# Attention, mixture of experts and dense layer in one kernel: early weight fetches, scales a task ahead, and a split on GpSimd

## The chip, the cores and the metric

One core of a Trainium2 chip runs the whole kernel in one launch. The metric is the device time of a run in microseconds (us); the median of the runs counts. A profile is one more execution, recorded instruction by instruction.

## The reference

Three layers follow each other. `a` below is a softmax of `phi` over the sequence.

```python
k_m, v_m = einsum('bhsm,bhsd->bhmd', a, k), einsum('bhsm,bhsd->bhmd', a, v)   # 8 x 8 heads, 576 x 64, 32 slots
x = softmax(q @ k_m.T / 8) @ v_m                    # -> x: 4608 tokens x 512
logits = x @ w_gate                                 # 8 experts, 576 tokens each, greedy by order of logits
out[mask_e] = relu(x[mask_e] @ w1[e]) @ w2[e]       # w1 512 x 1024, w2 1024 x 512, float32
h = out @ w_in;  g = h * clip(h + 3, 0, 6) / 6      # w_in 512 x 2048
y = g @ w_out                                       # w_out 2048 x 512
```

The expert that is filled first is chosen by the data, so its weights can be fetched only once the routing has found its index.

## The kernel before, in words

**Precision.** Matmuls run in float16 with each float32 operand split in a high and a low half (`hi = fp16(s*x)`, `lo = fp16(s*x - hi)`), three products for one. Weights and activations are first multiplied by a power of two found from their squares or their maximum.

**Stages.** The attention runs to about 240 us. Then the experts come in the order in which the routing finds them: `route(k)` is a chain of small steps between DVE and PE that ends in `ei{k}` (row numbers of the expert's weights) and `ix{k}` (its tokens). `gathers()` fetches the tokens' rows of x by five indirect DMAs from GpSimd and transposes them into `xt`. `l1(k)` and `l2(k)` are the expert's layers, 192 matmuls of 288 columns each. The result `y` (two tiles [128, 2, 576]; 512 columns are used here, the other 64 of all eight experts are collected into a ninth group) goes through `ysplit(k)`, and `unit(k)` is the dense layer of that group in eight steps: seven products `pq`/`pr` of six matmuls with 256 columns, then four pieces `acc` of six matmuls with 512 columns. The order is l1(0), l2(0), l1(1), l2(1), units 0 and 1, l1(2), l2(2), l1(3), l2(3), unit 2 and so on to units 6, 7 and 8.

**Weights of the experts.** `weights()` goes through 16 tasks T = 2k + which (which = 0: w1, 1: w2). For each it fetches four tiles `wst0` to `wst3` of [128, 1024] float32 by indirect DMA from GpSimd (`w_issue`), squares them on ACT, finds the scale (`pow2`), waits until the layer of the expert before no longer needs the float16 tiles, and converts eight halves: ACT writes the high half, DVE the low half (of three halves in tasks 1 to 3 GpSimd writes the low one, `PS`). As a tile is converted, `w_later` fetches the next task into it.

**Dense weights.** w_in and w_out arrive as 64-bit numbers. `dense_max()` takes the maximum of the last blocks, `dense()` loads 32 pieces in the order `PO` into buffers `dst` and rebuilds float32 numbers from them: ACT one or two copies, DVE two or three integer steps, paced by `turn()`. Pairs of w_in pieces become one of eight blocks `wid` in DRAM (`wino_weights`: sums on DVE, splits on ACT and GpSimd, two writes `wga`, `wgb`), which `stream()` reads back as `ws` for every step of every unit. w_out pieces become the resident tiles `wo` in slots 16 to 31.

**Order.** The instructions of each engine are put in order by a planner: generators wait for planned times and conditions while PE's work advances the clock `CK.now`; `V_`, `A_` and `G_` stand for DVE, ACT and GpSimd with a planned time `t`; `spawn(task, lim)` lets a task go on when its engine is planned to be free within `lim` us. The planner decides the order alone; on the chip each engine runs its list and waits for data.

**`ysplit(k)`** takes the maximum of y, finds a scale `s`, forms four sums of quarters of y on DVE (unscaled), and of seven operands writes the high half on ACT (`scale=s`) and the low half on DVE (`(src*s) - hi`).

Of the kernel before, what the change touches and what calls it, by code (L numbers as in the profile page):

```python
# [8 lines left out]
F32 = mybir.dt.float32  # L9
# [10 lines left out]
def attn_moe_kernel(ctx: ExitStack, tc: tile.TileContext, q, k, v, phi, w_gate, w1, w2, w_in, w_out, out):  # L20
# [677 lines left out]
    nc.gpsimd.iota(pb, pattern=[[1, 4]], base=512 * E, channel_multiplier=4, allow_small_or_imprecise_dtypes=True)  # L698
    tid = rt.tile([128, NT], I32, name="tid")
# [53 lines left out]
    IDX, EIX, SX = {}, {}, {}  # L753
# [14 lines left out]
    def route(k):  # L768
# [145 lines left out]
        EIX[k] = ei  # L914
        yield V_.t - 0.3
# [106 lines left out]

    def w_later(T, c):
        yield V_.t + HOP, G_
        w_issue(T, c)

    def weights():
        for T in range(2 * E):
            k, which = divmod(T, 2)
            while k not in EIX:  # L1030
                yield CK.now + 0.3
            for c in range(4):
                w_issue(T, c)
                yield CK.now + 0.8, G_
            while not XD[0]:
                yield CK.now + 0.1
            sq = rt.tile([128, 4], F32, name="wsq", bufs=2)
            for c in range(4):
                st, ready = WST[T, c]
                yield ready, A_  # L1040
                scr = wk.tile([128, 1024], BF16, name="wscr")
                A_.activation(scr, st, AF.Square, accum_out=sq[:, c:c + 1])
# [8 lines left out]
            (S1, S2)[which][k] = s  # L1051
            while k and (L1D, L2D)[which].get(k - 1, 0) < (8, 4)[which]:
                yield CK.now + 0.3
            tl, rd = [], []
            for n in range(9):
                if (k > 3 or T == 4) and n:
                    yield CK.now + (3.0 if k > 3 else 1.2), A_
                if n < 8:
# [3 lines left out]
                    cs = slice(i * 512, i * 512 + 512)  # L1062
                    if n in PS.get(T, ()):
                        A_.activation(WST[T, c][0][:, cs], WST[T, c][0][:, cs], AF.Copy, scale=s[:, 0:1])
                        yield A_.t - 0.3
                        A_.activation(tl[c][:, 0, cs], WST[T, c][0][:, cs], AF.Copy)
                    else:
                        A_.activation(tl[c][:, 0, cs], WST[T, c][0][:, cs], AF.Copy, scale=s[:, 0:1])
                    rd.append(A_.t + HOP)
                if n and n - 1 in PS.get(T, ()):  # L1070
                    yield rd[n - 1], G_
                    c, i = divmod(n - 1, 2)
                    cs = slice(i * 512, i * 512 + 512)
                    G_.tensor_tensor(tl[c][:, 1, cs], WST[T, c][0][:, cs], tl[c][:, 0, cs], op=OP.subtract)
                    yield (CK.now + 0.1, A_) if k > 1 else max(CK.now + 0.1, V_.t - 0.5)
                    WC[T] = c + i, tl
                elif n:
                    yield (rd[n - 1], V_) if k > 1 else rd[n - 1]
                    c, i = divmod(n - 1, 2)
                    cs = slice(i * 512, i * 512 + 512)  # L1080
# [720 lines left out]
```

## Time and profile before

| | |
|---|---|
| median of 3 runs | 1469.22 us (1468.58 to 1472.0) |
| profiled execution | 1465.18 us, span 1463.40 us |
| PE busy | 1335.5 us (91%) |
| DVE, ACT, POOL busy | 949.7 (65%), 818.9 (56%), 484.6 us (33%) |
| mean granted TensorE clock | 0.972 of full speed |
| DMA | 206.29 MB, mean 141 GB/s |

PE is TensorE, DVE VectorE, ACT ScalarE, POOL GpSimd, SP SyncE. Line L568 is the wrapper that issues nearly every instruction of DVE, ACT and POOL after the attention, L622 the one for matmuls, so groups are told apart by their tiles: `w<-wst` is a conversion, `wscr<-wst` a square, `p` an expert layer, `pq`, `pr` and `acc` a unit, `h` the activations of a layer or a unit, `cv`, `cva`, `wga`, `wgb`, `wo` the dense weights. In brackets a timeline gives the idle time before an instruction and what ended it.

### The profile page before, as it was taken

The page shows a single profiled execution, that of the slowest core. Times are in us where ns is not written, and L with a number is a line of the kernel's source. Part 1 is how long each engine was busy: PE and PEld are TensorE (multiplying, and loading weights), DVE is VectorE, ACT ScalarE, POOL GpSimd, SP SyncE. Part 2 cuts the span into 40 slices and gives each one's busy share as a digit, 9 for nine tenths or more (in the row PEclk, how much of TensorE's full clock was granted, in tenths as well). Part 3 has the DMA queues.
Part 4 walks back from the last instruction along what each step waited for, and adds up shares of the span by engine and source line. Part 5 has one row for each costly group of instructions (what it writes and reads, how often), then busy time and mean ns, then how long its engine had stood idle before and what let it go on. Part 6 is the DMA issues. An engine that isn't in the chain of part 4 may idle for free.

```text
span 1463.4 us, 27894 instructions
## 1 busy us (share of the span) xinstructions
PE 1335.5 (91%) x11132; PEld 1001.6 (68%) x11132; DVE 949.7 (65%) x2232; ACT 818.9 (56%) x1560; POOL 484.6 (33%) x530
## 2 busy tenths in 40 slices
PE   4778886987999999989899999999999999999998
PEld 3667665866765667877568767876786687666664
DVE  4687975778898888885875687476246424435322
ACT  3667655468687455554654565465437524545543
POOL 5775312145353343302332323323212211232323
PEclk9989997899999999999999999999999999999999
DMA  9984487446773353313332333234223202243321
GB/s 296 309 273 144 158 263 247 145 142 240 248 236 150 109 183 109 104 60 113 109 133 88 119 105 134 91 109 147 81 66 119 101 30 75 81 144 116 107 99 54
DMA packets 83490, 206.29 MB, mean 141 GB/s; under 512 B 11040, under 2 KB 41760, under 8 KB 83360
## 3 DMA queue, kind: packets, MB, share of 16 engines
q1 hardware_dynamic: 68192, 151.55, 30.6%
q0 software_dynamic: 15168, 52.96, 11.1%
q8 instruction: 87, 1.43, 0.4%
q14 instruction: 43, 0.35, 0.1%
HBM read 177.23 MB, written 27.26 MB: 140 GB/s over the span
## 4 chain that ended last, share of the span: by engine, by line
PE 56%; DVE 6%; issue 5%; ACT 2%; DMA 1%; POOL 1%; POOLq 0%; SPq 0%; ACTq 0%
PE acc L622 21%; PE p L622 16%; PE pq L622 10%; PE pr L622 8%; DVE h L568 1%; ACT h L568 1%; DMA wst<-in_moe_w_dram,ei 1%; PE xp L627 1%; DVE w L568 1%; DVE B L568 0%; DVE C L568 0%; PE rtp L838 0%; POOL h L568 0%; DMA ws<-wid 0%; POOL out_dram L568 0%
## 5 line engine op out<-in xcount | busy, mean ns | idle before, releaser
L622 PE MATMUL acc<-wo,h 128*128 128x512 f16 x1728 | 425.0, 380 | 0.3 <-DVE wo L568 0.2
L622 PEld LDWEIGHTS <-w 128*128 128x128 f16 x3072 | 338.2, 122 | 70.8 <-DVE w L568 8.1
L622 PEld LDWEIGHTS <-ws 128*128 128x128 f16 x3024 | 292.2, 98 | 109.8 <-issue 24.4
L568 POOL TENSOR_TENSOR h<-h,h 128x512 f16<-128x512 f32 x144 | 176.6, 1232 | 425.1 <-ACT h L568 300.5
L622 PEld LDWEIGHTS <-h 128*128 128x128 f16 x1728 | 166.3, 98 | 138.7 <-issue 2.3
L622 PE MATMUL p<-h,w 128*128 128x288 f16 x1536 | 206.2, 290 | 10.9 <-DVE w L568 3.9
L622 PE MATMUL p<-xt,w 128*128 128x288 f16 x1536 | 209.3, 291 | 7.3 <-POOL w L568 2.2
L568 ACT ACTIVATE h<-h,half_c,inv 128x512 f32<-128x512 f32 x144 | 116.5, 811 | 175.4 <-DVE h L568 147.3
L568 DVE SCALAR_TENSOR_TENSOR h<-h,h 128x512 f32<-128x512 f32 x144 | 102.4, 713 | 69.8 <-ACT h L568 69.5
L568 ACT ACTIVATE h<-pq,swv 128x256 f32<-128x256 f32 x216 | 101.4, 470 | 63.7 <-PE pq L622 60.4
L568 POOL DMA_INDIRECT wst<-in_moe_w_dram,ei x64 | 65.2, 1018 | 190.7 <-ACT y L568 50.5
L568 ACT ACTIVATE h<-p 128x288 f16<-128x288 f32 x128 | 52.3, 409 | 127.5 <-PE p L622 126.0
L568 DVE SCALAR_TENSOR_TENSOR h<-pr,swv,h 128x256 f32<-128x256 f32 x144 | 69.1, 480 | 84.1 <-PE pr L622 78.1
L568 DVE SCALAR_TENSOR_TENSOR h<-p,h 128x288 f16<-128x288 f32 x128 | 57.5, 453 | 67.9 <-ACT h L568 64.6
L568 DVE SCALAR_TENSOR_TENSOR w<-wst,s,w 128x512 f16<-128x512 f32 x119 | 97.3, 825 | 1.1 <-ACT w L568 1.1
L568 ACT ACTIVATE h<-h 128x512 f16<-128x512 f32 x144 | 89.4, 621 | 8.3 <-DVE h L568 8.2
L568 ACT ACTIVATE w<-wst,s 128x512 f16<-128x512 f32 x119 | 82.7, 712 | 5.7 <-DVE s L568 5.7
L568 ACT ACTIVATE wscr<-wst 128x1024 bf16<-128x1024 f32 x64 | 67.4, 1053 | 15.3 <-DMA wst<-in_moe_w_dram,ei 14.9
L568 ACT ACTIVATE y<-p 128x288 f32<-128x288 f32 x64 | 25.5, 409 | 87.5 <-PE p L622 79.9
L568 DVE TENSOR_REDUCE ym<-y 128x1 f32<-128x288 f32 (+1 forms) x66 | 30.7, 472 | 62.0 <-ACT y L568 61.7
L568 POOL DMA_INDIRECT xg<-xd,ix x35 | 35.9, 1027 | 102.2 <-DVE ix L568 44.5
L568 POOL DMA_INDIRECT out_dram<-y,ix x36 | 36.7, 1019 | 83.1 <-ACT y L568 79.3
(550 smaller groups left out, 2194.3 us busy)
## 6 DMA issues: line engine op xcount, KB each, us to landing
ws<-wid SPq DMA_DIRECT2D x72, 896.0 KB, 4.6
dst<-in_moe_w_out_dram SPq DMA_DIRECT2D x28, 512.0 KB, 5.3
qt<-in_q_dram SPq DMA_DIRECT2D x8, 1024.0 KB, 13.2
dq<-in_moe_w_in_dram SPq DMA_DIRECT2D x16, 512.0 KB, 4.8
xd<-xs SPq DMA_DIRECT2D x32, 256.0 KB, 5.5
dst<-in_moe_w_in_dram SPq DMA_DIRECT2D x16, 512.0 KB, 4.3
kvt<-in_k_dram SPq DMA_DIRECT2D x7, 1152.0 KB, 11.3
kvt<-in_v_dram SPq DMA_DIRECT2D x7, 1152.0 KB, 12.4
```

What stands on the lines that cost most here:

```text
L568: r = f(*a, **kw)
L622: nc.tensor.matmul(o, l, r, start=start, stop=stop, skip_group_check=more)
L627: nc.tensor.transpose(o, i, idn)
```

## The change

Tasks 1, 2 and 3 are fetched by a task of their own, `w_first`. Tasks 1 and 3 (w2 of experts 0 and 1) go as eight half tiles [128, 512] into slots 24 to 31, the room of w_out's last eight tiles; a new index tile `e8` addresses half rows. Task 2 (w1 of expert 1) uses the four `wst` tiles. The squares and scales of all tasks become a task `scales()`, and `weights()` only converts. In `ysplit` y is multiplied by `s` in place on DVE (two instructions); the high halves are plain copies, and for all groups but the first the sums and low halves go to GpSimd. Three loads of dense blocks are issued by GpSimd instead of SyncE; `dense_max` and `dense` start when the gathers of expert 0 are issued, not at the first eviction of xt; pieces of w_out from the ninth on wait until w2 of expert 1 is converted; and some planned times change.

```diff
+            e8 = rt.tile([128, 8], I32, name="e8", bufs=2)
+            V_.scalar_tensor_tensor(e8, cm.to_broadcast([128, 8]), -1024.0, pb8, op0=OP.mult, op1=OP.add)
...
     def w_issue(T, c):
-        if k not in EIX or (T, c) in WST:
+        if k not in EIX or (T, c) in WST or T in (1, 2, 3):
             return
...
+    def w_first():
+        for T in (1, 2, 3):
+            while not (XR if T == 1 else W1 if T == 2 else W2):
+                yield CK.now + 0.1
+            while not (0 in XI if T == 1 else 1 in EIX if T == 2 else 1 in XI):
+                yield CK.now + 0.1
+            for n in range(4 if T == 2 else 8):
+                yield CK.now, G_
+                c, i = divmod(n, 2)
+                if T == 2:
+                    st = wk.tile([128, 1024], F32, name=f"wst{n}")
+                    G_.indirect_dma_start(out=st, out_offset=None, in_=wv[0], in_offset=U(ap=EIX[1][:, n:n + 1], axis=0))
+                    WST[T, n] = st, dma(1.5, G_.t)
+                else:
+                    st = slot(24 + n, [128, 512], F32, f"wsh{n}_")
+                    G_.indirect_dma_start(out=st, out_offset=None, in_=w28,
+                                          in_offset=U(ap=EI8[T // 2][:, n:n + 1], axis=0))
...
-    def weights():
+    def scales():
         for T in range(2 * E):
...
+            before = T - 1 if T > 4 else T - 2
+            def free(c):
+                return T < 4 or WC.get(before, (0,))[0] > c
...
+            hf = 2 if T in (1, 3) else 1
...
-                yield ready, A_
+                yield ready + (2.5 if 0 < T < 4 else 0.0), A_
...
+                        A_.activation(scr[:, i * 512:i * 512 + 512], w_src(T, 2 * c + i), AF.Square,
+                                      accum_out=sq[:, 2 * c + i:2 * c + i + 1])
...
+    def weights():
+        for T in range(2 * E):
+            k, which = divmod(T, 2)
+            while k not in (S1, S2)[which]:
+                yield CK.now + 0.1
...
-        dense_fetch(st, 16 * which + j)
+        dense_fetch(st, 16 * which + j, nc.gpsimd if NEM < DN[0] < NEM + 4 else nc.sync)
...
     def dense_max():                                   # and in dense()
-        while not GI[0]:
+        while 0 not in XI:
...
-            while not (SDR[which] and spare(1)):
+            while not (SDR[which] and spare(1)) or which and j > 7 and 1 not in W2:
                 yield CK.now + 0.2
-            spawn(dense_piece(which, j, *dload(which, j)), 0.1)
+            spawn(dense_piece(which, j, *dload(which, j)), 0.5 if NB[0] == 4 else 0.1)
...
     def turn():
-        while CK.now < TURN[0] or V_.t > CK.now + 0.05:
+        while CK.now < TURN[0] or V_.t > CK.now + (0.5 if NB[0] == 4 else 0.05):
             yield max(TURN[0], CK.now + 0.05)
-        TURN[0] = CK.now + (1.15 if NB[0] == 4 else 0.85)
+        TURN[0] = CK.now + 0.85
...
-                XDT[0] = dma(0.73, A_.t)
+                XDT[0] = dma(0.73, A_.t) + 1.5
...
-        spawn(ysplit(k), 0.8)
+        spawn(ysplit(k), 0.8 if k else 2.0, k == 0)
...
+        for y in (ya, yb):
+            V_.tensor_scalar(y[:, :, 0:512], y[:, :, 0:512], s, None, op0=OP.mult)
...
-        V_.tensor_tensor(x1, t2, u2, op=OP.add)
-        V_.tensor_tensor(x2, x1, t1, op=OP.subtract)
-        V_.tensor_tensor(t2, t1, t2, op=OP.subtract)
-            A_.activation(ST[k][i][:, 0], src, AF.Copy, scale=s)
-                V_.scalar_tensor_tensor(t[:, 1], src, s, t[:, 0], op0=OP.mult, op1=OP.subtract)
+        Q_ = G_ if k else V_
+        def half(i, src, r):
+            yield r, A_
+            A_.activation(ST[k][i][:, 0], src, AF.Copy)
+            yield A_.t + HOP, Q_
+            Q_.tensor_tensor(ST[k][i][:, 1], src, ST[k][i][:, 0], op=OP.subtract)
+            nl.add(i)
...
+            Q_.tensor_tensor(o, p, q, op=op)
+            spawn(half(i, o, Q_.t + HOP), 0.8 if k else 2.0, k == 0)
...
     spawn(gathers())
+    spawn(scales(), 0.6)
     spawn(weights(), 0.6)
+    spawn(w_first(), 0.6)
```

## Rows read from the trace of the kernel before

**Rows 1.** The page's 40 slices of the span, TensorE, busy tenths
```profile
PE   4778886987999999989899999999999999999998
```

**Rows 2.** Windows: busy us (and count) of each engine per stretch, clock, DMA
```profile
core 0: us, PE busy (x) PEld busy (x) DVE busy (x) ACT busy (x) POOL busy (x), PEclk, DMA share, GB/s
...
260.00:280.00 20.00, 19.79 (x249) 16.90 (x250) 13.87 (x44) 7.23 (x16) 2.22 (x2) 0.87 0.50 164
...
320.00:340.00 20.00, 14.87 (x104) 11.24 (x105) 18.64 (x34) 15.52 (x29) 12.22 (x11) 0.92 0.71 246
...
400.00:420.00 20.00, 19.41 (x134) 13.12 (x134) 19.76 (x37) 18.49 (x37) 12.79 (x10) 1.00 0.85 278
...
420.00:440.00 20.00, 18.94 (x129) 12.52 (x128) 19.55 (x32) 17.52 (x33) 9.49 (x9) 1.00 0.66 218
...
sum 190.00, PE 171.22 PEld 134.26 DVE 164.00 ACT 135.79 POOL 77.18; mean PE 17.12 PEld 13.43 DVE 16.40 ACT 13.58 POOL 7.72
```

**Rows 3.** Timeline of PE, 290 to 390 us: start, us, what, [idle before, releaser]
```profile
298.54 4.77 PE L622 MATMUL p<-h,w 128*128 128x288 f16 x24 [2.36 <-DVE h L568]
...
330.49 0.99 PE L622 MATMUL p<-xt,w 128*128 128x288 f16 x6
...
337.51 3.75 PE L622 MATMUL p<-xt,w 128*128 128x288 f16 x18 [2.21 <-POOL w L568]
...
341.32 20.13 PE L622 MATMUL p<-xt,w 128*128 128x288 f16 x163
...
364.90 0.66 PE L622 MATMUL p<-h,w 128*128 128x288 f16 x2 [3.24 <-ACT w L568]
...
386.54 0.82 PE L622 MATMUL pq<-st__4930,ws 128*128 128x256 f16 x6
```

**Rows 4.** Timeline of POOL (GpSimd): fetches of weights and rows, 290 to 345 us
```profile
297.64 0.96 POOL L568 DMA_INDIRECT wst<-in_moe_w_dram,ei  x1 [1.39 <-DVE sl L568]
...
304.53 0.94 POOL L568 DMA_INDIRECT wst<-in_moe_w_dram,ei  x1 [0.30 <-issue]
...
311.44 1.09 POOL L568 DMA_INDIRECT xg<-xd,ix  x1 [4.78 <-DVE ix L568]
...
332.25 0.97 POOL L568 DMA_INDIRECT wst<-in_moe_w_dram,ei  x1
```

**Rows 5.** Timeline of ACT: first dense piece, first square, conversions of expert 1
```profile
278.98 0.79 ACT L568 ACTIVATE sgn<-dst 128x512 f16<-128x512 f32 x1
...
308.43 1.06 ACT L568 ACTIVATE wscr<-wst 128x1024 bf16<-128x1024 f32 x1 [7.89 <-DMA wst<-in_moe_w_dram,ei]
...
325.12 0.71 ACT L568 ACTIVATE w<-wst,s 128x512 f16<-128x512 f32 x1
...
364.14 0.71 ACT L568 ACTIVATE w<-wst,s 128x512 f16<-128x512 f32 x1
```

**Rows 6.** Chain that ended last, 440 to 470 us: start, us, what
```profile
451.95 2.30 DMA wid<-wgb
454.39 4.37 DMA ws<-wid
458.81 0.83 PE pq L622 x6
```

**Rows 7.** Timeline of SP (SyncE): last writes of x, then dense loads
```profile
236.41 2.51 SPq L429 DMA_DIRECT2D xd<-xs  x3
239.02 2.46 SPq L76 DMA_DIRECT2D dst<-in_moe_w_out_dram  x2
242.45 0.38 SPq L74 DMA_DIRECT2D dst<-in_moe_w_in_dram  x1
```

**Rows 8.** Groups of DVE instructions, 400 to 450 us: busy us, mean ns
```profile
L568 DVE TENSOR_TENSOR sx__5747<-y,sx__5748 128x512 f32<-128x512 f32 x1 | 1.6, 1647 | 0.0
...
L568 DVE SCALAR_TENSOR_TENSOR st__5741<-y,sy,st__5741 128x512 f16<-128x512 f32 x1 | 0.7, 735 | 0.0
...
L568 DVE TENSOR_TENSOR sx__5747<-y,y 128x512 f32<-128x512 f32 x1 | 0.7, 684 | 0.0
```

**Rows 9.** Timeline of POOL, 416 us: the low half of h
```profile
416.10 1.16 POOL L568 TENSOR_TENSOR h<-h,h 128x512 f16<-128x512 f32 x1 [1.81 <-ACT h L568]
```

**Rows 10.** Timeline of PE, 423 us: matmuls that use that h
```profile
423.44 1.46 PE L622 MATMUL acc<-wo,h 128*128 128x512 f16 x6
```

**Rows 11.** Waits of PE over the span: us, times, longest
```profile
PE pr L622 <- DVE h L568: 10.9, 8, 2.6
```

More of the change, by code (lines that the diff above doesn't have):

```diff
@@ L751, in absmax @@
         return m
-    IDX, EIX, SX = {}, {}, {}
+    IDX, EIX, EI8, SX = {}, {}, {}, {}
     SR = [False]
@@ L1031, in weights @@
                 yield CK.now + 0.3
+            before = T - 1 if T > 4 else T - 2
+            def free(c):
+                return T < 4 or WC.get(before, (0,))[0] > c
             for c in range(4):
[L1033 to L1037, printed above, removed]
+                if c == 2:
+                    while not XD[0]:
+                        yield CK.now + 0.1
+                if free(c):
+                    w_issue(T, c)
+                    yield CK.now + 0.8, G_
+            hf = 2 if T in (1, 3) else 1
+            sq = rt.tile([128, 8], F32, name="wsq", bufs=2)[:, 0:4 * hf]
             for c in range(4):
+                while (T, c) not in WST:
+                    if free(c):
+                        w_issue(T, c)
+                    yield CK.now + 0.1
                 st, ready = WST[T, c]
-                yield ready, A_
+                yield ready + (2.5 if 0 < T < 4 else 0.0), A_
                 scr = wk.tile([128, 1024], BF16, name="wscr")
-                A_.activation(scr, st, AF.Square, accum_out=sq[:, c:c + 1])
+                for i in range(hf):
+                    if hf == 2:
+                        A_.activation(scr[:, i * 512:i * 512 + 512], w_src(T, 2 * c + i), AF.Square,
+                                      accum_out=sq[:, 2 * c + i:2 * c + i + 1])
+                        A_.t += 0.15
+                    else:
+                        A_.activation(scr, st, AF.Square, accum_out=sq[:, c:c + 1])
                 yield (CK.now + 3.0, A_) if k > 3 else A_.t + (0.3 if T else -0.1)
@@ L1051, in weights @@
             (S1, S2)[which][k] = s
+    def weights():
+        for T in range(2 * E):
+            k, which = divmod(T, 2)
+            while k not in (S1, S2)[which]:
+                yield CK.now + 0.1
+            s = (S1, S2)[which][k]
             while k and (L1D, L2D)[which].get(k - 1, 0) < (8, 4)[which]:
@@ L1540, in ysplit @@
         ST[k] = [slot(7 * (k % 2) + i, [128, 2, 2, 256], F16, f"st{i}_") for i in range(7)]
-        nl = [0]
+        nl = set()
         x1, x2 = (slot(14 + i, [128, 2, 256], F32, f"sx{i}_") for i in range(2))
-        V_.tensor_tensor(x1, t2, u2, op=OP.add)
-        r1 = V_.t + HOP
-        yield V_.t + 0.5, V_
-        V_.tensor_tensor(x2, x1, t1, op=OP.subtract)
-        r2 = V_.t + HOP
-        yield V_.t + 0.5, V_
-        V_.tensor_tensor(t2, t1, t2, op=OP.subtract)
-        r3 = V_.t + HOP
-        for i, src, r in ((A11, t1, 0.0), (A12, u1, 0.0), (A22, u2, 0.0), (S1Y, x1, r1), (S2Y, x2, r2), (S3Y, t2, r3),
-                          (S4Y, x1, 0.0)):
-            if i == S4Y:
-                V_.tensor_tensor(x1, u1, x2, op=OP.subtract)
-                r = V_.t + HOP
-            yield (max(r, CK.now + (0.9 if k == 2 else 2.0)), A_) if k > 1 else (max(r, CK.now + 2.0 * k), A_)
-            A_.activation(ST[k][i][:, 0], src, AF.Copy, scale=s)
-            def low(t=ST[k][i], src=src):
-                yield (A_.t + HOP, V_) if k > 1 else A_.t + HOP
-                V_.scalar_tensor_tensor(t[:, 1], src, s, t[:, 0], op0=OP.mult, op1=OP.subtract)
-                nl[0] += 1
-            spawn(low(), 0.8)
-            while i in (S1Y, S4Y) and nl[0] < (4, 7)[i == S4Y]:
-                yield CK.now + 0.1
+        Q_ = G_ if k else V_
[5 more added lines that the diff above has]
+            nl.add(i)
+        r = V_.t + HOP
+        for i, src in ((A11, t1), (A12, u1), (A22, u2)):
+            spawn(half(i, src, r), 0.8 if k else 2.0, k == 0)
+            yield CK.now + 0.7, Q_
+        for i, o, p, q, op in ((S1Y, x1, t2, u2, OP.add), (S2Y, x2, x1, t1, OP.subtract), (S3Y, t2, t1, t2, OP.subtract),
+                               (S4Y, x1, u1, x2, OP.subtract)):
+            while i == S4Y and S1Y not in nl:
+                yield CK.now + 0.1
+            yield CK.now, Q_
+            Q_.tensor_tensor(o, p, q, op=op)
+            spawn(half(i, o, Q_.t + HOP), 0.8 if k else 2.0, k == 0)
+            yield Q_.t, Q_
+        while len(nl) < 7:
+            yield CK.now + 0.1
         YR[k] = True
```

28 lines of the change are left out of this document (22 added, 6 removed).

## The prediction

> **What bounds the kernel now.** I read the page's slices first [rows 1]. TensorE (PE) stands at nine tenths or more in every slice of the last third, so nothing there can give much time back; the sixes, sevens and eights lie, but for two, in the first ten slices of 36.6 us, and the attention, which the change leaves alone, takes seven of these. Then I read the stretch behind it window by window [rows 2]: from 320 us on VectorE (DVE) is as full as PE, 19.76 and 19.55 of 20 us at 400 to 440, while between 260 and 280 us it is busy for only 13.87. Over 260 to 450 us it is busy for 164.0 of 190 us, so 26.0 us are free, nearly all before 400.
>
> PE's timeline says what each stage loses [rows 3]. The undisturbed pace is 163 matmuls in 20.13 us, 0.1235 us each. The second layer of expert 0 waits 2.36 us for an eviction on DVE, and its next 24 matmuls take 4.77 us where the pace gives 2.96. The first layer of expert 1 runs from 330.49 to 361.45 us, 30.96 us for 192 matmuls that need 23.7: 7.2 us too long, with a wait on a weight half that GpSimd writes. The second layer of expert 1 then waits 3.24 us for its first converted weights; its 144 matmuls ahead of the dense part need 17.8 us, and the dense part starts at 386.54, 25.1 us after the first layer ended: 7.3 too long.
>
> The weight rows show why [rows 4, 5]. All weights go through one set of four staging tiles, so expert 1's w1 is fetched at 297.64 to 305.5 us, ScalarE (ACT) stands 7.89 us waiting for its landing, and conversion starts at 325.12; w2 of expert 1 is fetched only after that, 332.25 to 341.9, and converted from 364.14.
>
> Last the chain around 450 us [rows 6]: the eighth block of dense-layer weights is written at 451.95, read back at 454.39, and PE gets it at 458.81. So PE runs unit 0 into the end of a second pipeline, the rebuilding of w_in on DVE. Whatever PE gains before 386 us counts only if this pipeline ends earlier too.
>
> **The change part by part.**
>
> *Fetches of tasks 1, 2, 3.* w2 of experts 0 and 1 go into eight half tiles in w_out's slots, w1 of expert 1 into the four staging tiles, free since expert 0's w1 was converted. Task 2's four issues, spread over 7.8 us by waits for these tiles, would take 4 x 1.26 = 5.0 (0.96 busy, 0.30 to the next [rows 4]), and the first no longer stands behind task 1's conversion: I take its landing 6 us earlier (3 to 10). Task 3 no longer waits for task 2's conversion: it follows expert 1's five gathers, which start at 311.44, so it leaves at about 311.44 + 5 x 1.26 = 317.7 instead of 332.25. The price is eight half fetches for four, twice: 8 x 1.26 = 10.1 us of GpSimd time, in a stretch where it is mostly idle (2.22 of 20 us busy at 260 to 280) [rows 2]. What queues behind them on GpSimd are the low halves of w1's conversion, and these have until 330.
>
> *Scales a task ahead.* Squares and power-of-two scale of the next task no longer wait for the conversion of the one before. Eight half squares replace four, twice: each costs between half of a square's 1.06 us and all of it [rows 5], so a task's take 4.2 to 8.5 us instead of 4.2; I take a conversion's 0.71 of the same width, 5.7, 1.5 more, hidden in the time in which ACT waits there now.
>
> *What PE gets back.* Second layer of expert 0: 2.36 + 1.81 = 4.2, I take 4. First layer of expert 1: 7.2, I take 6, since its rows, gathered from 311.44 on, must still land and be copied twice, and are next late. Second layer of expert 1: 7.3, I take 5.5; task 3 issued from 317.7, with task 2's own 10.8 us from first issue to first square and 16.7 from there to conversion [rows 4, 5], converts from about 345, or 350 with the doubled fetches, and the first layer would end at 361.45 - 4 - 6 = 351. Sum 15.5 us at the start of unit 0 (bounds 5 and 19).
>
> *Dense pieces.* Pieces start once the gathers are issued, look 0.5 us ahead instead of 0.05, and follow each other after 0.85 instead of 1.15 us while only four banks serve the expert layers. Their first ACT step is now at 278.98 [rows 5]. Which part of DVE's 26.0 idle us this fills cannot be read off: none at worst, since many gaps are answers awaited from PE; all of it at best. I take a third, 8.7, because the gaps before 320 us are the large ones but belong partly to the routing of expert 1.
>
> *Three loads moved from SyncE to GpSimd.* They leave at 239.02 to 242.8 today, among the last writes of x [rows 7], and the gather of x waits for those writes. On GpSimd they come after the gathers. I take 1 us for the earlier gather (0 to 3). Their issue on GpSimd is not shown: between SyncE's 0.38 and an indirect issue's 1.26 us, at most 3.8 us on an idle engine.
>
> *y scaled in place and split on GpSimd.* For expert 1, in the full stretch 400 to 432, DVE loses four sums and seven low halves: 4 x 0.68 + 7 x 0.74 = 7.9 us [rows 8]. It gains two in-place scalings of 128x1024, not shown before: between 0.68 (a 512-wide row) and twice that, I take 1.0 each. Expert 0 keeps its sums on DVE and pays 2 x 1.0 less 7 x 0.06 = 1.6 us more. The eleven moved instructions cost about 1.16 us each on GpSimd, the length of the h split there [rows 9]: 12.8 us per expert, off the path: unit 1 needs them after the eight blocks of unit 0, whose last starts 72 us after the first [rows 3, 6]. What queues behind them on GpSimd is the low half of h: it ended at 417.26 and the matmuls that use it come some 7 us later, after four of the six matmuls starting at 423.44 [rows 9, 10], so a delay of one or two instructions stays covered.
>
> One thing speaks against this part. On DVE the sum of two SBUF tensors takes 0.684 us in one place and 1.647 in another of the same shape [rows 8], and the long ones lie beside GpSimd instructions. The Trainium skill (SBUF — State Buffer, "Who interferes with whom") says that a DVE instruction with two SBUF inputs and a GpSimd instruction that reads SBUF exclude each other for the whole instruction; by it, eleven more GpSimd instructions could take back up to 12.8 us of DVE time per expert, more than the 7.9 moved. The trace agrees with the lengthening. I count 1.5 us for expert 1 (0 to 11 x 0.96 = 10.6), since only some DVE instructions there have two SBUF inputs. Relief: 7.9 - 2.0 - 1.5 = 4.4 us.
>
> *The sum.* PE's side is 15.5 us earlier at unit 0. The dense side is 8.7 + 4.4 - 1.6 = 11.5 us earlier at the eighth block, and that is the smaller, so it decides; with the gather 12.5. After 470 us, DVE's relief for the later experts touches the 10.9 us in which PE waits for h on DVE [rows 11]: I take 1.5, less 0.5 for collisions. Together 13.5 us. The profiled execution took 1465.18 us (span 1463.40): it becomes 1451.7. The median of the runs is 4.0 us above it, so I forecast 1456 us.
>
> **The rivals.**
>
> *A, the dense pipeline does not move.* DVE's idle time is latency, the relief is eaten by collisions, and PE comes 15 us early to wait at the eighth block. For it: DVE at 99% in [rows 2] and the chain in [rows 6]. Against: the first piece at 278.98 has 40 us of half-empty DVE around it. Only the late 1.5 and the gather stay: 1467 us.
>
> *B, slower: GpSimd locks DVE in the units.* Eight splits (experts 1 to 7 and the leftover one) put 88 instructions beside DVE's joins and products, from 402 us to the end. If one in three holds a DVE instruction for the 0.96 us seen and PE waits for it, 88 x 0.3 x 0.96 = 25 us come back: 1481 us. From 14 such cases on, the whole gain is gone. For it: the lengthened rows in [rows 8], PE's waits on h in [rows 11]. Against: the 7 us of cover in [rows 9, 10], and that the same splits sit on DVE itself today. The exclusion that the Trainium skill states (SBUF — State Buffer, "Who interferes with whom") would be its cause.
>
> *C, more: both pipelines come forward fully.* The stages lose no wait and the dense pieces fill more than half of the idle 26 us: PE's 19 and 5 more from DVE's relief later on, 1445 us or a little below.
>
> **How the numbers follow.** Forecast 0.53, A 0.15, B 0.17, C 0.15. About 0.3%, 4.4 us, is what a measurement of this kernel can tell from no change: faster means below 1464.8, slower above 1473.6. The forecast's own range is 1448 to 1464, nearly all of it faster (0.51, 0.02 the same). A is mostly the same (0.09), in part faster (0.05); 0.01 of it slower. B is slower with 0.15, the same with 0.02. C is all faster. Faster 0.71, same 0.13, slower 0.16. The range reaches from below C to just short of B: 1441 to 1477, with about 0.2 outside.
>
> **What would show it.** Right: no ACT wait of several us for expert 1's w1; its conversion starting near 315 and that of w2 near 350; unit 0 starting near 371 instead of 386.54; the last of the eight dense blocks written near 440 instead of 451.95; DVE fuller before 320 us and below 19 of 20 us at 400 to 440. Wrong: unit 0 early but its eighth step still at 455 or later (A); DVE products of two SBUF tensors over 1 us on average, and PE waits on DVE h above 11 us (B); conversions of expert 1 that start no earlier, because the routing of expert 1 slid behind the early dense pieces, would take the PE side of the sum away.

## The result, and the profile after

The changed kernel took 1486.9 us in the median of four runs (1479.6 to 1487.6), against 1468.9 us for the kernel before beside it (1468.3 to 1472.0): a ratio of 1.0107, 95% interval 1.0072 to 1.0142. It is slower; I had forecast 1456 us, and the time lies above the range. The profiled execution took 1486.16 us with a span of 1484.3, 20.9 more than before.

The slices of the page, TensorE, answer to [rows 1]. The twelfth and thirteenth slice, 408 to 482 us (37.1 us each), read 7 and 8 where [rows 1] has nines; behind them only the 24th and 27th read 8 for 9, and the last 7 for 8.
```profile
PE   4778886978978999989899989989999999999997
```
The windows of after, columns as in [rows 2], whose last three stretches they answer. GpSimd (POOL), the last column before the clock, goes from 9.49 to 20.00 of 20 us at 420 to 440, and PE loses 3 us there, while DVE is hardly relieved (19.55 to 18.77). At 320 to 340 all engines but GpSimd do less than before.
```profile
320.00:340.00 20.00, 12.90 (x76) 9.34 (x75) 10.84 (x21) 12.41 (x22) 15.73 (x15) 0.83 0.72 244
...
400.00:420.00 20.00, 17.34 (x118) 11.38 (x117) 19.34 (x34) 15.44 (x31) 13.20 (x12) 1.00 0.83 252
420.00:440.00 20.00, 15.99 (x108) 10.38 (x107) 18.77 (x23) 16.59 (x30) 20.00 (x16) 0.99 0.53 202
```
PE's timeline of after answers to [rows 3]: unit 0 starts at 386.71, as before (386.54). Expert 1's first layer starts 5.0 us later (335.53 for 330.49), behind a new wait of 4.17 us for gathered rows, and its two layers together win back 4.9. Inside unit 0 PE then waits 5.54 us for a block of w_out, which no row of before showed.
```profile
327.73 1.09 PE L627 MATMUL xp<-ident,xg 128*128 128x128 f32 x4 [4.17 <-DMA xg<-xd,ix]
...
335.53 1.32 PE L622 MATMUL p<-xt,w 128*128 128x288 f16 x8
...
364.28 0.53 PE L622 MATMUL p<-h,w 128*128 128x288 f16 x3
...
386.71 0.82 PE L622 MATMUL pq<-st__5034,ws 128*128 128x256 f16 x6
...
441.53 1.86 PE L622 MATMUL acc<-wo,h 128*128 128x512 f16 x4 [5.54 <-DVE wo L568]
```
The gather, and ACT's first dense piece and conversions, answer to [rows 4, 5]. The first piece is 19 us earlier, but the conversions of expert 1 only 5.4 and 6.1 us, and its gather is 7.6 us later (318.99 for 311.44).
```profile
318.99 0.97 POOL L568 DMA_INDIRECT xg<-xd,ix  x1 [7.29 <-DVE ix L568]
```
```profile
259.70 0.79 ACT L568 ACTIVATE sgn<-dst 128x512 f16<-128x512 f32 x1 [1.59 <-DMA dst<-in_moe_w_in_dram]
...
319.70 0.71 ACT L568 ACTIVATE w<-wst,s 128x512 f16<-128x512 f32 x1
...
358.06 0.74 ACT L568 ACTIVATE w<-wsh__4750,s 128x512 f16<-128x512 f32 x1
```
GpSimd's timeline of after, where [rows 9] had one h split with 1.81 us of idle time before it: sums (sx) and low halves (st) of expert 1 stand between h and the dense blocks (wga), back to back for 25 us. The splits took 1.16 to 1.72 us each.
```profile
419.79 1.34 POOL L568 TENSOR_TENSOR h<-h,h 128x512 f16<-128x512 f32 x1
421.09 1.72 POOL L568 TENSOR_TENSOR sx__5810<-sx__5809,y 128x512 f32<-128x512 f32 x1
422.78 1.15 POOL L568 TENSOR_TENSOR wga<-cva,wga 128x512 f16<-128x512 f32 x1
...
438.67 1.60 POOL L568 TENSOR_TENSOR st__5807<-y,st__5807 128x512 f16<-128x512 f32 x1
440.23 1.60 POOL L568 TENSOR_TENSOR st__5808<-sx__5809,st__5808 128x512 f16<-128x512 f32 x1
441.79 1.15 POOL L568 TENSOR_TENSOR wga<-cva,wga 128x512 f16<-128x512 f32 x1
```
DVE's timeline beside it, against the short and long forms of one shape in [rows 8]: h products at 1.64 and two in 3.20, where one at 415.60 took 0.67.
```profile
415.60 0.67 DVE L568 SCALAR_TENSOR_TENSOR h<-h,h 128x512 f32<-128x512 f32 x1
...
417.33 2.78 DVE L568 TENSOR_TENSOR cva<-cva 128x256 f32<-128x256 f32 x2 [0.46 <-POOL wga L568]
420.04 1.64 DVE L568 SCALAR_TENSOR_TENSOR h<-h,h 128x512 f32<-128x512 f32 x1
...
437.61 3.20 DVE L568 SCALAR_TENSOR_TENSOR h<-h,h 128x512 f32<-128x512 f32 x2
```
The chain that ended last, around the eighth block (start us, us, what), answers to [rows 6]: the read of this block starts at 465.41 instead of 454.39.
```profile
437.69 3.12 DVE h L568 x2
440.81 0.67 DVE wo L568
441.53 1.86 PE acc L622 x4
...
465.41 4.42 DMA ws<-wid
```
PE's waits over the span [rows 11]: the one on h is about as long as before (10.6 for 10.9 us), though DVE was to be relieved; the one on w_out is new.
```profile
PE pr L622 <- DVE h L568: 10.6, 8, 3.1
...
PE acc L622 <- DVE wo L568: 6.4, 3, 5.5
```

### The profile page after: what moved, and what is told of

The parts are those of the page before. It is cut to its first block, busy times and chain, and to the rows that moved or that the text cites. A ratio compares the mean times of both kernels' runs of the same rounds, so it can differ in the third digit from the quotient of the medians.

```text
span 1484.3 us, 27922 instructions
## 1 busy us (share of the span) xinstructions
PE 1345.8 (91%) x11132; PEld 1006.1 (68%) x11132; DVE 949.0 (64%) x2167; ACT 814.2 (55%) x1573; POOL 605.3 (41%) x631
## 4 chain that ended last, share of the span: by engine, by line
PE 62%; DVE 18%; ACT 5%; DMA 5%; issue 4%; POOL 3%; SPq 1%; another core or an unknown queue 0%; POOLq 0%; DVEq 0%; ACTq 0%
PE p L622 19%; PE acc L622 19%; PE pq L622 9%; PE pr L622 7%; DVE h L568 2%; DMA wst<-in_moe_w_dram,ei 2%; PE xa L419 2%; ACT h L568 2%; DVE w L568 2%; PE kvp L190 1%; DVE ql L329 1%; DMA kvt<-in_v_dram 1%; DMA xg<-xd,ix 1%; PE xp L627 1%; DVE C L568 1%
## 5 line engine op out<-in xcount | busy, mean ns | idle before, releaser
L568 POOL TENSOR_TENSOR h<-h,h 128x512 f16<-128x512 f32 x144 | 172.9, 1206 | 331.3 <-ACT h L568 217.6
L568 ACT ACTIVATE h<-h,half_c,inv 128x512 f32<-128x512 f32 x144 | 116.5, 811 | 163.6 <-DVE h L568 141.2
L568 DVE SCALAR_TENSOR_TENSOR h<-h,h 128x512 f32<-128x512 f32 x144 | 114.7, 800 | 69.3 <-ACT h L568 68.8
L568 ACT ACTIVATE h<-pq,swv 128x256 f32<-128x256 f32 x216 | 101.2, 469 | 76.1 <-PE pq L622 73.0
L568 DVE SCALAR_TENSOR_TENSOR h<-pr,swv,h 128x256 f32<-128x256 f32 x144 | 69.2, 481 | 93.1 <-PE pr L622 80.9
L568 ACT ACTIVATE h<-p 128x288 f16<-128x288 f32 x128 | 51.9, 408 | 123.6 <-PE p L622 121.1
L568 POOL DMA_INDIRECT wst<-in_moe_w_dram,ei x56 | 54.4, 972 | 152.5 <-DVE ei L568 70.8
L568 DVE SCALAR_TENSOR_TENSOR h<-p,h 128x288 f16<-128x288 f32 x128 | 57.8, 453 | 66.6 <-ACT h L568 63.3
L568 DVE SCALAR_TENSOR_TENSOR w<-wst,s,w 128x512 f16<-128x512 f32 x109 | 96.2, 888 | 3.3 <-ACT w L568 3.2
L568 ACT ACTIVATE h<-h 128x512 f16<-128x512 f32 x144 | 89.3, 620 | 10.1 <-DVE h L568 9.9
L568 ACT ACTIVATE w<-wst,s 128x512 f16<-128x512 f32 x109 | 76.1, 712 | 7.8 <-DVE s L568 7.8
L568 POOL DMA_INDIRECT xg<-xd,ix x35 | 35.9, 1025 | 101.3 <-DVE ix L568 57.3
L568 ACT ACTIVATE wscr<-wst 128x1024 bf16<-128x1024 f32 x56 | 59.0, 1054 | 31.1 <-DMA wst<-in_moe_w_dram,ei 30.8
L568 POOL DMA_INDIRECT out_dram<-y,ix x36 | 36.4, 1011 | 84.3 <-ACT y L568 73.0
L568 ACT ACTIVATE y<-p 128x288 f32<-128x288 f32 x64 | 25.4, 407 | 81.4 <-PE p L622 63.9
L568 DVE TENSOR_REDUCE ym<-y 128x1 f32<-128x288 f32 (+1 forms) x66 | 30.7, 472 | 56.6 <-ACT y L568 56.3
```

The lines of the kernel that those rows point to most:

```text
L568: r = f(*a, **kw)
```

## The experiments

The ratios are to the kernel before, run beside each on the same chip (medians of before there: 1467.0 to 1469.9 us). "Unit 0" is the time from its first product to that of unit 1, "units 1 to 4" from there to the first product of unit 5, both of the profiled execution. That of the kernel before took 1465.18 us, 2 to 5 us less than its medians here. In every run but e1, e2 and e5 the planner also orders the rest of the kernel anew.

| kernel | median us | ratio, 95% | unit 0 starts | unit 0 | units 1 to 4 |
|---|---|---|---|---|---|
| before | 1468.9 | | 386.5 | 83.7 | 617.1 |
| after | 1486.9 | 1.0107 (1.0072–1.0142) | 386.7 | 92.9 | 627.6 |
| e1 after, no split on GpSimd | 1461.5 | 0.9957 (0.9939–0.9976) | 382.1 | 89.9 | 607.5 |
| e2 after, low halves twice | 1518.4 | 1.0339 (1.0306–1.0372) | 381.9 | 100.7 | 646.3 |
| e3 after, split on DVE | 1489.7 | 1.0146 (1.0120–1.0172) | 385.7 | 99.6 | 618.6 |
| e4 after, y part undone | 1468.6 | 1.0003 (0.9985–1.0021) | 384.7 | 84.5 | 617.3 |
| e5 after, memsets for splits | 1463.7 | 0.9967 (0.9949–0.9985) | 378.5 | 91.8 | 612.9 |
| e6 before + fetches | 1474.0 | 1.0030 (1.0016–1.0044) | 381.9 | 101.8 | 612.6 |
| e7 before + dense pieces | 1450.8 | 0.9874 (0.9847–0.9901) | 386.6 | 78.9 | 609.7 |
| e8 after, no priority | 1480.0 | 1.0080 (1.0050–1.0109) | 386.9 | 81.7 | 630.8 |
| e9 before + y part | 1480.5 | 1.0084 (1.0060–1.0107) | 385.7 | 90.8 | 629.1 |
| e10 before + fetches + dense | 1482.5 | 1.0100 (1.0075–1.0125) | 407.0 | 82.0 | 615.6 |
| e11 before + dense + loads | 1460.7 | 0.9953 (0.9934–0.9972) | 393.4 | 78.8 | 610.0 |
| e12 before + early gate | 1468.4 | 1.0002 (0.9990–1.0015) | 387.5 | 83.8 | 620.7 |
| e13 e7 + fetch of task 3 | 1458.9 | 0.9930 (0.9907–0.9952) | 392.5 | 82.1 | 606.7 |
| e14 before + pace | 1453.1 | 0.9895 (0.9863–0.9927) | 388.3 | 78.9 | 606.6 |
| e15 e7, faster pace | 1473.2 | 1.0030 (1.0012–1.0048) | 397.7 | 83.0 | 612.4 |

### The y part: e1, e2, e5, e3, e4, e8, e9

The y part is what the change does to `ysplit`: scaling in place, plain copies, the split on GpSimd, and expert 0's split ahead of the dense pieces. In e1, e2 and e5 PE, DVE, ACT and SP issue what they issue in the kernel after, in its order (the planner is charged the same cost); only GpSimd's list differs. e1 and e5 leave out the sums and low halves, so they do not compute the layer, and some of their copies and products read another tile.

*e1:*
```
-            Q_.tensor_tensor(ST[k][i][:, 1], src, ST[k][i][:, 0], op=OP.subtract)
+            G_.cost([128, 512])      # k > 0; likewise for the sums
...
-                    mm(banks[b][0], wt[:, blk, wi, c], ST[k][x][:, xi, c], ...
+                    mm(banks[b][0], wt[:, blk, wi, c], ST[k][x][:, 0 if k else xi, c], ...
```


> The kernel after, every instruction of the other engines in the same order, without GpSimd's 88 split instructions (11 for each of experts 1 to 7 and the leftover one): ScalarE still writes the high halves, the products read the high half in place of the low one, the sums are left out. Theory G (GpSimd's new work holds up DVE and GpSimd's own low halves of h and of w_in): most of the loss comes back, 1470 to 1476 us; GpSimd is busy for about 10 of 20 us at 420 to 440 us instead of 20.0; the pairs of w_in's last step take 0.9 us instead of 2.8; the last products of unit 0 start near 460 instead of 469.87; mean of DVE's products of two SBUF tensors back from 800 to about 710 ns. Rival O (the order of the dense pieces and of expert 1's routing is worse, whoever does the splits): 1483 to 1488 us, unit 0 still ends near 479.

*e2:*
```
             Q_.tensor_tensor(ST[k][i][:, 1], src, ST[k][i][:, 0], op=OP.subtract)
+            if k:
+                nc.gpsimd.tensor_tensor(ST[k][i][:, 1], src, ST[k][i][:, 0], op=OP.subtract)
```


> The kernel after with each of the seven low halves of a split issued twice on GpSimd (56 instructions of about 1.16 us more), nothing else changed in any engine's order. Theory G: GpSimd is already full at 420 to 440 us, so unit 0 loses some 8 us more and the later units 1 to 2 us each: 1496 to 1508 us. Rival O: the work is off the path, 1485 to 1490 us.

*e5:*
```
-            Q_.tensor_tensor(ST[k][i][:, 1], src, ST[k][i][:, 0], op=OP.subtract)
+            for n in (256, 256, 128):      # k > 0; likewise for the sums
+                nc.gpsimd.memset(ST[k][i][:, 1, :, 0:n], 0.0)
```


> The kernel after, all orders kept, with each of the 88 split instructions on GpSimd replaced by three memsets (640 values a partition wide each time, no input): the low halves are zero and the sums are left out. GpSimd is about as busy with the splits as in the kernel after (88 x some 1.3 us), but these instructions read nothing. If the loss is the lock (GpSimd's reading instructions and DVE's two-SBUF ones exclude each other): near e1_nosplit, 1461 to 1468 us, mean of DVE's products h<-h,h near 715 ns. If it is GpSimd's queue (low halves of h and of w_in late behind the split): near the kernel after, 1480 to 1490 us, with the means of DVE back but the same waits of PE for GpSimd's halves.

The same group of DVE (L575 is L568 moved by added lines), its 144 products of two SBUF tensors, in e1, e5, after and e2 (busy us, mean ns, then idle time before them):
```profile
L575 DVE SCALAR_TENSOR_TENSOR h<-h,h 128x512 f32<-128x512 f32 x144 | 103.1, 718 | 77.1 <-ACT h L575 76.8
```
```profile
L575 DVE SCALAR_TENSOR_TENSOR h<-h,h 128x512 f32<-128x512 f32 x144 | 103.6, 721 | 79.7 <-ACT h L575 79.1
```
```profile
L568 DVE SCALAR_TENSOR_TENSOR h<-h,h 128x512 f32<-128x512 f32 x144 | 114.7, 800 | 69.3 <-ACT h L568 68.8
L568 DVE SCALAR_TENSOR_TENSOR h<-pr,swv,h 128x256 f32<-128x256 f32 x144 | 69.2, 481 | 93.1 <-PE pr L622 80.9
```
```profile
L568 DVE SCALAR_TENSOR_TENSOR h<-h,h 128x512 f32<-128x512 f32 x144 | 125.1, 873 | 89.6 <-ACT h L568 89.3
```
And the busy line of the page of e1, e5 and after:
```profile
PE 1332.2 (91%) x11132; PEld 1001.4 (69%) x11132; DVE 895.4 (61%) x2167; ACT 814.6 (56%) x1573; POOL 487.8 (33%) x543
```
```profile
PE 1338.6 (92%) x11132; PEld 1003.8 (69%) x11132; DVE 902.4 (62%) x2167; ACT 813.6 (56%) x1573; POOL 605.7 (41%) x807
```
```profile
PE 1345.8 (91%) x11132; PEld 1006.1 (68%) x11132; DVE 949.0 (64%) x2167; ACT 814.2 (55%) x1573; POOL 605.3 (41%) x631
```
With the same 2167 DVE instructions, DVE is busy for 895.4 us without splits, 902.4 beside memsets that keep GpSimd as busy as in after, and 949.0 beside splits that read SBUF. So GpSimd's reading lengthens DVE's work by 46.6 us, and being busy, without reading, by 7.0. DVE's form with one operand in PSUM (pr) stays at 480 ns in all. In time e1 gave back more than expected, e2 cost more, and e5 came out as expected for the lock: within 2.2 us of e1 and 23 us below after. Some of these 23 us are not the splits': up to expert 1's split at 417 us the streams are the same, and yet unit 0 starts 4.6 to 8.2 us earlier in e1, e2 and e5 than in this one execution of after. In it PE stood at the lower of its two granted clocks (0.50 of full speed) from 327.0 to 333.8 us, behind the wait of 4.17 us, and DVE stood for 6.15 us until 265.68, as in e1 and e2 (6.5 and 6.2 us) but not in e5 (2.5 us at most).

From the start of unit 0 to that of unit 5, the reading costs 1.1 + 14.7 = 16 us against e5, and 23 against e1; a second copy of the low halves costs 26 more (e2). So the loss against e5 lies behind unit 0. There PE is idle for 33.0 of 627.4 us in after and for 21.8 of 612.7 in e5, and the wait on h has little part in it. PE's waits in this stretch, first of after, then of e5, are spread over many places; waits on a step of the routing (C) and on converted weights (w) are among those that grew:
```profile
PE pr L622 <- DVE h L568: 8.4, 7, 3.1
...
PE rtp L840 <- DVE C L568: 3.0, 4, 1.4
PE p L622 <- DVE w L568: 2.5, 1, 2.5
```
```profile
PE pr L629 <- DVE h L575: 7.7, 6, 2.4
...
PE rtp L847 <- DVE C L575: 1.4, 1, 1.4
```
e5's memsets need not wait for ACT's high halves, so they may also sit better in GpSimd's queue; its split into reading and waiting is not finer than that. That the added work only costs GpSimd's queue is refuted by e5, and that this order is bad without the splits' work by e1.

*e3:* `Q_ = V_` for all experts.

> The kernel after with the sums and low halves of all experts on DVE, as they were, the in-place scaling kept. Theory G: the lock is gone but DVE gets 11 x 0.7 us per expert back; unit 0's loss mostly comes back, 1470 to 1478 us. Rival O: 1483 to 1490 us, since the dense pipeline and the routing stay as they are.

Theory G missed: no better than after, and inside the range of rival O, which e1 refutes in its turn. Units 1 to 4 take 618.6 us, 9 less than in after. Unit 0 takes 99.6, 6.7 more; that this is because DVE, full there, now has the sums and low halves in a burst (the pauses of 0.9 to 2 us between them are gone) and the in-place scalings (18, 14.8 us in all) as well is argued, not shown. With the split on DVE in its old form e4 (below) is only 7 us above e1, which leaves the split's work out. So the new form is dear on DVE as well, where GpSimd reads nothing for it; by which of its steps no run shows. The busy lines of the pages say how little GpSimd takes over: DVE is busy for 963.1 us in e3, 949.0 in after and 895.4 in e1. Of 68 us that the split costs DVE, 54 stay when GpSimd does it.

*e4:* the functions of the y part as before:
```
-        spawn(ysplit(k), 0.8 if k else 2.0, k == 0)
+        spawn(ysplit(k), 0.8)
...
-        for y in (ya, yb):
-            V_.tensor_scalar(y[:, :, 0:512], y[:, :, 0:512], s, None, op0=OP.mult)
...
+            A_.activation(ST[k][i][:, 0], src, AF.Copy, scale=s)
```


> The kernel after with the y part undone as a whole (scale fused into the split again, split on DVE, its old place in the queue): the fetches, the scales a task ahead, the three loads and the early dense pieces alone. Theory G: these keep what the prediction gave them in part, 1455 to 1468 us. Rival O: 1480 us or more, because they are what put unit 0 late; rival W (the fetches do not come forward): 1467 to 1472 us.

The y part costs 18 us (1486.9 to 1468.6), the whole loss; what remains of the change gains nothing. The time lies in rival W's range, but not for W's reason: conversions of expert 1 do come forward (319.21 and 357.03 us). Rival O is refuted.

*e8:* `0.8 if k else 2.0, k == 0` becomes `0.8` in the three spawns of the split.

> The kernel after with expert 0's scaling and split back at their old place in the planner's list (behind the dense pieces, 0.8 us ahead instead of 2.0); all else as after. In e1_nosplit the third to eighth dense blocks are 5 to 10 us later than in e4_no_y although nothing is split on GpSimd there: if that comes from expert 0's split at 345 to 362 us ahead of the dense pieces, this kernel gets 4 to 7 us back, 1480 to 1483 us; if it comes from the in-place scaling or the order at large, 1485 to 1489 us.

As expected, 7 us: unit 0 takes 11 us less (92.9 to 81.7), units 1 to 4 take 3 more (630.8) and keep their loss. With expert 0's split ahead of them the dense pieces are late and fall into expert 1's split on GpSimd: the low halves of the sixth block come at 430.42 in after, in the midst of that split, and in e8 at 413.33, before it begins at 415.08. Not all of this is the split's place: the first block's low halves, made before expert 0's split, are already 3.4 us earlier in e8 (306.21 for 309.60).

*e9:* the y part alone in the kernel before (the reverse of e4's diff).

> The kernel before with the y part alone (scaled in place, expert 0's split on DVE ahead of the dense pieces, the others' on GpSimd). From the kernel after against e4_no_y it costs 18 us there: if it does so for itself, 1481 to 1492 us, DVE's products h<-h,h at 770 to 810 ns on average instead of 713, and the loss lies both in unit 0 and between 480 and 1090 us. Rival (it hurts only where the dense pieces have been moved too): 1466 to 1474 us.

12 us slower by itself (0.0084 x 1467), a little less than expected, in unit 0 (90.8) and in units 1 to 4 (629.1); the mean of h products is 792 ns.

### The other parts: e6, e7, e10 to e15

*e6:*
```
+    spawn(scales(), 0.6)
     spawn(weights(), 0.6)
+    spawn(w_first(), 0.6)
...
+            while not (...) or which and j > 7 and 1 not in W2:
```


> The kernel before with the fetches of tasks 1 to 3 into the room of w_out and the scales a task ahead alone (and the wait that keeps w_out's pieces out of that room). My prediction gave this part 15.5 us at the start of unit 0, not at the end: 1462 to 1469 us if the dense pieces hold the eighth block where it is; unit 0 starts at 371 to 380 us instead of 386.54. Rival (nothing comes forward, because routing of expert 1 and its gather set the end of expert 0's second layer): unit 0 at 384 to 388 us, 1466 to 1472 us.

Slower than either expectation: unit 0 starts only 4.7 us earlier and takes 18 us longer. PE's timeline answers to [rows 3]:
```profile
331.92 1.51 PE L622 MATMUL p<-xt,w 128*128 128x288 f16 x11
...
356.60 0.90 PE L622 MATMUL p<-h,w 128*128 128x288 f16 x6
358.81 11.19 PE L622 MATMUL p<-h,w 128*128 128x288 f16 x90 [1.31 <-DVE h L568]
374.30 7.71 PE L622 MATMUL p<-h,w 128*128 128x288 f16 x48 [4.31 <-ACT y L568]
381.85 0.82 PE L622 MATMUL pq<-st__5027,ws 128*128 128x256 f16 x6
```
The fetches do what they were to do: expert 1's gather is where it was (311.61), and its conversions start at 313.49 and 345.35, not 325.12 and 364.14. Its first layer takes 24.8 us instead of 31.0. But that layer starts 1.4 us later than before, so expert 0's second layer won nothing, and expert 1's second layer takes 25.1 us as before, with waits on h (DVE) and y (ACT) in place of the wait on weights.

In unit 0, 400 to 484 us, PE's waits are on w_out's conversion, and the low halves of the eighth block begin at 455.43 instead of 450.14. Those of the first block are late too (329.77 for 322.34): GpSimd makes them 4.7 us after ACT's high halves have ended at 325.07, with the eight issues from 318.93 to 332.68 around them. By the sixth block this delay is down to 1.4 us (413.43 for 412.07), so it does not explain the eighth. That expert 1's earlier squares and conversions pass the pieces is argued from the order, not shown.
The waits:
```profile
PE acc L622 <- ACT wo L568: 12.2, 3, 6.2
PE acc L622 <- DVE wo L568: 3.6, 2, 2.5
```
*e7:*
```
-        while not GI[0]:
+        while 0 not in XI:
...
-            spawn(dense_piece(which, j, *dload(which, j)), 0.1)
+            spawn(dense_piece(which, j, *dload(which, j)), 0.5 if NB[0] == 4 else 0.1)
...
-        while CK.now < TURN[0] or V_.t > CK.now + 0.05:
+        while CK.now < TURN[0] or V_.t > CK.now + (0.5 if NB[0] == 4 else 0.05):
...
-        TURN[0] = CK.now + (1.15 if NB[0] == 4 else 0.85)
+        TURN[0] = CK.now + 0.85
```


> The kernel before with the early dense pieces alone (gate at the issued gather, 0.5 us of look-ahead, 0.85 us between steps while four banks serve the experts). My prediction gave 8.7 us at the eighth block: 452 to 443 us, and 1463 to 1469 us. Rival (they only push the routing of expert 1 back): eighth block at 450 us or later, l2(0) ends 2 us or more later, 1468 to 1475 us.

Better than expected, and the best kernel of all: 1.3% faster than before. GpSimd's timeline: the low halves of the eighth block are made at 436.24, 13.9 us earlier than before (450.14). Unit 0 starts where it did and takes 4.8 us less, units 1 to 4 take 7.4 less; what makes these shorter no row shows.
```profile
436.24 1.79 POOL L568 TENSOR_TENSOR wgb<-cva,wgb 128x512 f16<-128x512 f32 x2 [3.14 <-issue]
```
*e12, e14:* e7's early start alone (the first edit), and its look-ahead and pace alone (the others).

> The kernel before with one of the edits of the dense pieces alone: they start when expert 0's gathers are issued; look-ahead and pace stay at 0.05 and 1.15 us. If the early start makes e7_before_dense's gain of 19 us: 1449 to 1457 us. If it is the pace and the look-ahead: 1463 to 1470 us, with the last of the eight blocks at 446 us or later.

> The kernel before with the look-ahead of 0.5 us and the pace of 0.85 us alone, without the early gate. The gate alone (e12) left every stage within 1 us of before up to the end of unit 0, so the pace makes the gain: 1448 to 1454 us. Rival (only both together do): 1462 us or more.

The gate alone does nothing; look-ahead and pace make the gain (e14 within 0.2% of e7).

*e15:* `0.85` becomes `0.6` and `0.5` becomes `0.8` while four banks serve the experts.

> e7_before_dense with a look-ahead of 0.8 us and a pace of 0.6 us while four banks serve the experts. If the dense pieces still have room between the routing's steps: 1440 to 1449 us, eighth block before 436 us. If VectorE has no more gaps there: 1449 to 1458 us, expert 1's routing later by 2 us or more.

0.3% slower than before, and slower than either expectation. The pieces go by (the eighth block's low halves at 433.16), but PE waits 7.8 us for the scale of expert 1's w2 (PE's waits, 300 to 400 us), and unit 0 starts at 397.7.
```profile
PE amx L722 <- DVE s_1m L568: 7.8, 1, 7.8
```
*e10, e11:* e7 with the edits of e6; e7 with `nc.gpsimd if NEM < DN[0] < NEM + 4 else nc.sync` (and 1.5 us on `XDT[0]`).

> The kernel before with the fetches, the scales a task ahead and the early dense pieces: e4_no_y without the three loads moved to GpSimd. e7_before_dense took 1450.8 us, e6_before_fetch 1474.0 and the three parts together 1468.6. If the moved loads hold the dense pieces back: 1448 to 1456 us, the second block at 320 to 330 us instead of 350. If it is the fetches (they push the routing of expert 1 and the second pair of pieces back): 1464 to 1472 us, second block near 350.

> The kernel before with the early dense pieces and the three loads on GpSimd, without the fetches. If the loads hold the pieces back: 1460 to 1470 us, second block near 350 us. If it is the fetches: 1448 to 1453 us, as with the dense pieces alone, second block near 322.

Both add to e7's time: the loads some 10 us, the fetches some 32, though with both (e4) it is 18. e11 stands at the edge of what was expected if the loads hold the pieces back, but its second block comes at 331.95, not near 350. e10's comes at 351.21, as expected if it is the fetches, but the time is 10 us above that range. Neither expectation names the place in e10: there PE, DVE and ACT stand together for 10.6 us, PE for DVE's step FL, ACT for PE, and DVE for 12.05 us in all. PE's timeline: the 36 matmuls of the routing end at 254.5, DVE's step that follows them comes only at 266, and within that time GpSimd issues expert 0's eight half fetches (253.9 to 263.6).
```profile
253.43 1.05 PE L830 MATMUL rtp<-Bo,C 128*15 128x8 bf16 x36
266.29 0.16 PE L860 MATMUL rtp<-FL,onesb 15*128 15x8 bf16 x1 [11.81 <-DVE FL L568]
```
And DVE's, where "remote" is a releaser that the profile does not tell:
```profile
266.08 0.15 DVE L568 TENSOR_SCALAR FL<-rtp 15x8 bf16<-15x8 f32 x1 [12.05 <-remote]
```
In after DVE stands for 6.15 us before the same step, and all three engines for 2.4 until 265.7; in e6, with the same fetches, they do not. What held DVE no row shows (the matmuls that FL reads had long ended); this stays open, and with it how much of e10's loss belongs to the fetches.

*e13:*
```
-        if k not in EIX or (T, c) in WST:
+        if k not in EIX or (T, c) in WST or T == 3:
...
+    spawn(w_first(), 0.6)      # for T in (3,)
```


> e7_before_dense with one fetch of the three: expert 1's w2 goes into the room of w_out as eight half tiles, and w_out's pieces 8 to 15 wait for its conversion; tasks 1 and 2 and all scales stay as before. If the fetch of task 1 at 253 us and the scales a task ahead are what costs: 1444 to 1453 us, with conversion of w2 of expert 1 near 355 instead of 364 us. If any fetch into this room costs (its eight issues on GpSimd, the wait of w_out's pieces): 1456 to 1470 us.

One fetch of the three costs 8 us, as expected if any fetch into this room costs; conversion of w2 starts at 370.21, not near 355. GpSimd's timeline: the eight issues stretch from 321.46 to 336.05, with two splits between them. The low halves of w1's conversion and of a dense block, at 326.77 and 322.35 in e7, come at 333.50 and 336.06. But the queue is not shown to hold them: for the first GpSimd stands idle for 2.51 us until ACT's high half is there, which ACT begins at 331.28 instead of 324.06, and ACT begins the high halves of the second at 333.93 instead of 321.64. What makes ACT late stays open.
```profile
321.46 0.95 POOL L568 DMA_INDIRECT wsh__4680<-in_moe_w_dram,e  x1 [0.30 <-issue]
...
333.50 1.16 POOL L568 TENSOR_TENSOR w<-wst,w 128x512 f16<-128x512 f32 x1 [2.51 <-ACT w L568]
334.81 1.24 POOL L568 DMA_INDIRECT wsh__4827<-in_moe_w_dram,e  x1
336.06 2.25 POOL L568 TENSOR_TENSOR wgb<-cva,wgb 128x512 f16<-128x512 f32 x2
```

## Why the prediction was wrong

The forecast was 13.5 us faster; the kernel is 18 slower. About 10 us of the miss lie in the fetches, dense pieces and loads, which together were to give 9.7 us and give nothing (e4), and about 22 in the y part, which was to give 3.8 and costs 18.

**What bounds the kernel.** Right in part: e6 brings PE 4.7 us forward for nothing, since unit 0 then ends later. But e7, with the blocks 13.9 us forward, ends unit 0 only 4.8 us earlier, as PE comes no earlier; the rest of its gain lies behind unit 0, in no term of mine.

**The fetches, 15.5 us on PE's side.** The conversions came forward as forecast where the fetches stand alone (e6), so not the fetch failed but two of the three terms that I hung on it. Expert 0's second layer, 4 us, gave -1.4; expert 1's first layer, 6 us, gave 6.1; its second layer, 5.5 us, gave 0.0, because other waits, on h and y, took the place of the wait on weights. That is 4.7 us, below my bound of 5. And a price was put at nothing: the eighth dense block comes 5.3 us later, so that the kernel is 4 us slower. I hid 10.1 us of issues under a GpSimd read as idle at 260 to 280 us, while half of them lie at 320 to 340, where [rows 2] already had it 12.22 of 20 us busy; this made the first block late, but is not shown to make the last one late. In after, with the dense pieces, the conversions came at 319.70 and 358.06 and the gather 7.6 us late, the sign that I had named as wrong; with either part alone it is at most 1.0 us late (e6, e7).

**The dense pieces, 8.7 us.** Right in sign, too small: the eighth block came 13.9 us earlier in e7, which gains 18.5 us by the medians (0.0126 x 1469.9) and 12.2 between the profiled executions. The idle time of DVE was usable for more than a third. Joined with the fetches the gain is gone. That both use the same gaps of DVE, ACT and GpSimd, which I added as if each had them to itself, fits e13 and e10 but is argued, and in e10 a stand of unknown cause has a part.

**The three loads, 1 us earlier.** With the dense pieces alone they cost some 10 us, with the fetches too they save 14 (e10 to e4), where DVE's stand is 6.67 us instead of 12.05. No sign of their own can be given.

**The y part, relief of 4.4 us at expert 1 and 1.5 later.** This is the term that made the kernel slower, and the step that failed is the price of the collisions behind unit 0. The in-place scaling was sized rightly (1.0 us, measured 0.975), and so, against e5, were the collisions in unit 0: 1.5 us counted, 1.1 measured (3.0 against e1). Behind it I counted 0.5 us, and 14.7 were measured up to unit 5 against e5, 20.1 against e1. I had looked there at PE's wait on h alone, which hardly changed; the loss is in other waits. The busy time of DVE shows the collisions without any argument on the path: 949.7 us before, 949.0 after, with 65 instructions fewer. What was taken from DVE came back as longer instructions and in-place scalings. Expert 0's split, priced at 1.6 us, cost some 7 through its place ahead of the dense pieces (e8, less what the first block had already gained).

**The rivals.** B named the mechanism and the price, 25 us, but had a chance of 0.17, and I let the range end before it. That its price is near the measured 16 to 23 us is partly luck: DVE lost 46.6 us to the reading, 0.53 per moved instruction where B took 0.29, about a third of it reached PE's time, and neither sign that I had named for B appeared (DVE's products average 0.800 us, not over 1; PE's wait on h is 10.6 us, not above 11). What spoke for B was in [rows 8], one shape at 0.684 and 1.647 us; what I set against it, that the splits sit on DVE today and that h has 7 us of cover, speaks of GpSimd's queue and not of DVE, whose instructions get longer. e5 settles between the two: the Trainium skill (SBUF — State Buffer, "Who interferes with whom") says that a DVE instruction with two SBUF inputs is held by GpSimd instructions that read SBUF and not by those that only write, and the trace agrees, 721 ns beside memsets and 800 beside splits.

## What to carry to other kernels

Moving elementwise work with SBUF operands from VectorE to GpSimd relieves VectorE by little where its remaining work has two SBUF inputs (here 14 of 68 us): before the move, count each moved instruction at its GpSimd length against VectorE's free time, and look at every wait on VectorE, not at one. When a fetch comes earlier, ask which wait ends last once the one on weights is gone. Price parts that fill the same gaps together. When a change has several parts, run each alone: here one part of four gives 1.3%, and the other three take it back and more.

## What the runs showed of the hardware

GpSimd's instructions lengthen as well: a split of 128x512 takes between 1.15 and 1.73 us in after; the 88 took 120.2 us, 1.37 each. DVE's in-place scaling of 128x1024, which has one SBUF tensor as input, takes 0.74 to 0.75 us while GpSimd is idle; where it started under a memset of e5, at 1105.5 and 1330.3 us, it took 0.96 and 1.03. So this form lengthens beside instructions that only write, too. And DVE stood for 12.05 us in e10, and PE and ACT with it, for a reason that no row names.
